# Sums of squares, transfer constants, weight layout and step sharing in a hand-scheduled attention and MoE kernel

## The chip, the cores and the metric

The kernel runs on one core of a Trainium2 chip. The metric is the device time of one execution in microseconds (us). TensorE (PE in the profile; PEld is its weight load) multiplies matrices, VectorE (DVE), ScalarE (ACT) and GpSimd (POOL) work element by element, and SyncE (SP) issues nearly all DMAs.

## The reference

For 8 batches, 8 heads, 576 positions and head size 64, q and k are mapped to 128 positive features, and linear attention is computed with them; its output goes through a feed-forward layer with an unusual gate.

```python
def phi(x):                                   # x is q or k, scaled by 64 ** -0.25
    proj = einsum('bhsd,md->bhsm', x, omega)
    sq = sum(x * x, axis=-1, keepdims=True) / 2.0
    h = proj - sq
    h = h - max(h, axis=-1, keepdims=True)
    return exp(h) / sqrt(m)
kv = einsum('bhsm,bhsd->bhmd', k_p, v);  z = sum(k_p, axis=2)
attn = einsum('bhsm,bhmd->bhsd', q_p, kv) / (einsum('bhsm,bhm->bhs', q_p, z)[..., None] + 1e-06)
h = x @ w_in                                  # x: 4608 x 512, w_in: 512 x 2048
g = h * erf(softplus(h))
out = g @ w_out                               # w_out: 2048 x 512
```

## The kernel before

The program is not written in the order in which it runs. `build` (from line 415) describes some thousands of operations: for each its name, the engines that may do it with a modelled cost and a slack for each, the tiles it reads and writes, and for some a planned time. `Plan.order` (line 161) then plays these operations through a model of the engines on the host, and the order that comes out on each engine is the order of its instructions on the chip. On the chip every engine works strictly in that order and waits where an input is not there yet, so an operation whose input is late holds everything behind it on its engine.

In the model an operation carries a due time, worked back from the planned times of the products that need it (and of the operations that need its buffers). Engines are tried in the order TensorE, ScalarE, VectorE, GpSimd, SyncE; each takes the ready operation that is due first. GpSimd takes a step that another engine may do as well only when it is due later than a slack. VectorE takes any. The names in `SHARED` (line 92) are the steps between VectorE and GpSimd: gates, splits into a high and a low part ("high", "rest"), sums of blocks and of weights, and the operands x. A DMA is modelled at lines 301 to 305: one transfer after the other at `RATE`, and landed a fixed time later. A weight fetch may be issued when it is due within `AHEAD`.

Batches follow one another. In each there are two phases (b, ph); in a phase four groups of first products (matmuls that write h, hA, hS) alternate with four of second products (o, in batches from 3 on bA and bS) of the phase before. From batch 2 on both layers use seven block products in place of eight. `starts` holds planned phase starts: 51 us for the first, then 64.5 us for each phase of batches 0 and 1, 61.3 us up to the first phase of batch 3, and 58.2 us from there on. In each phase 13.8 us are planned for attention of the next batch, spread between the products.

Attention of a batch is done for pairs of heads, two pairs (a quad) at a time. `load` (line 628) fetches u (transposed rows, for TensorE) and for each pair `un` (rows by position, 128 x 576, in one of two buffers). `un` is squared on ScalarE or GpSimd; `fold` (GpSimd, line 1200) adds halves and quarters of each row of 64 and scales, which leaves 144 numbers per partition; `sum_squares` (VectorE, line 1207) reduces these to 9 twice, once negated, into `sq`. In `project` (line 651) VectorE takes the maximum of the projection into a third place of `sq` and adds the three up (`shift`), which is the bias of the exponential on ScalarE. The first batch's pairs take another path (`load_pair`) without `fold`.

`split` (line 741) makes a batch's operands xh and xl from the attention's output, by way of differences xc; `chain` (line 873) runs softplus, erf and the gate; `operands` (line 905) makes the block operands (tiles T, gh_B, gl_B, gh_T, gl_T).

Weights are split once into high and low parts and stored in DRAM (`store`, line 458; tiles wdw, wdcSS, wdcST), then fetched into eight slots `w` of 512 KB. For the second layer a unit is stored by rows of blocks: the array is [partition, block row, block column, high or low, 256], so a row is 4 KB in one piece per partition. `column` (line 512) fetches a block column, two pieces of 2 KB (tiles wcA, wcS). `column_sums` (line 525) fetches rows (tile ct), forms sums (`make_sums`: RT, ST) and stores them again (cST to wdcST).

All instructions go through one helper, so every one has line 1064 in the profile; tiles tell them apart.

Of the kernel before, what the change touches and what calls it, by code (L numbers as in the profile page):

```python
# [11 lines left out]
F32 = mybir.dt.float32  # L12
# [6 lines left out]
ALU = mybir.AluOpType  # L19
# [4 lines left out]
P = 128  # L24
# [88 lines left out]
class Plan:  # L113
# [47 lines left out]
    def order(self, slots, caps):  # L161
# [67 lines left out]
        while True:  # L229
            progress = True  # L230
            while progress:
                progress = False
                for e in engines:
                    if not idle[e]:
                        continue
                    skipped, chosen = [], None
                    while ready[e]:
                        item = heapq.heappop(ready[e])
                        o = item[2]
                        if o.start is not None:  # L240
                            continue
                        ok = can(o)
                        if ok and e == "A":
                            if lock is not None and o.set is not None and o.macro != lock:
                                ok = False
                        if ok:
                            slack = next(s for x, _, s in o.opts if x == e)
                            if e == "S":
                                ok = o.due - now < slack
                            elif o.due - now + late < slack and slack > -1e8:  # L250
                                ok = False
                        if ok:
                            chosen = o
                            break
                        skipped.append(item)
                        if len(skipped) > 500:
                            break
                    for item in skipped:
                        heapq.heappush(ready[e], item)
                    if chosen is None:  # L260
                        continue
                    if e == "T" and half and chosen.half != half:
                        near = [x for x in ready[e] if x[2].half == half and x[2].start is None
                                and x[0] < now + NEAR and can(x[2])]
                        if near:
                            heapq.heappush(ready[e], (chosen.due, chosen.id, chosen))
                            chosen = min(near)[2]
                    o = chosen
                    progress = True
                    dur = next(c for x, c, _ in o.opts if x == e)  # L270
                    if e == "T":
                        if o.half != half:
                            dur += COST["turnout"] / 2
                        half = o.half
                        late += 0.1 * (max(0.0, now - o.due) - late)
                    if e == "V" and o.name in SHARED:

                        dur += max(0.0, until["G"] - now) % piece
                        port = now + dur
                    elif e == "G":  # L280
                        dur += max(0.0, port - now)
                        piece = dur / PIECES.get(o.name, 1) + 1e-6
                    o.eng, o.start = e, now
                    for t in o.alloc:
                        t.slot = free[t.pool].pop(0)
                        held[t.stream] += 1
                        nxt[t.stream] += 1
                    idle[e] = False
                    if e == "A":
                        if o.set is not None and o.set != table:  # L290
                            dur += COST["table"]
                            if o.set == "exp":
                                out.append("table")
                            table = o.set
                        if o.macro is not None:
                            lock = o.macro
                            if o.name.startswith("erf!"):
                                lock = None
                    out.append(o)
                    if e == "S":  # L300
                        event(now + 0.5, "idle", e)
                        begin = max(now, bw)
                        bw = begin + o.size / RATE
                        o.end = bw + 2.0
                    else:
                        o.end = until[e] = now + dur
                        event(o.end, "idle", e)
                    busy[e] += dur
                    event(o.end, "done", o)
# [43 lines left out]
        return out  # L353


RATE = 380e3
AHEAD = 40.0
AGAIN = 6
TURNS = tuple(range(0, 1000, 30))
REACH = 60.0  # L360
# [33 lines left out]
RESTS = 2.0  # L394
EARLY = (2, 0)
POW = 0
RECIP = 0.0
EARLYB = 7
PW = 1
# [15 lines left out]
def build(emit):  # L415
# [42 lines left out]
    def store(u, t):  # L458
        i = u[-1] if u[0] in "2T" else 0
        u_ = u[:-1] if u[0] in "2T" else u  # L460
        if u_ not in homes:
            homes[u_] = pl.tile("wd" + t.name, "wd" + t.name, [P, 2 if u[0] in "2T" else 1, *t.shape[1:]])
        d = homes[u_]
        stored[u] = (d, i)
        pl.op("wstore", [("S", 0.1, 1e9)], lambda e: E.fetch(d.ap[:, i], t.ap.bitcast(F32)),
              reads=[(t, (x, k)) for x in "hl" for k in range(2)], writes=[(d, i)],
              plan=clock[0] + 10.0, size=P * HW * 8)

# [30 lines left out]
    def unit(u, block=None):  # L499

        count[0] += 1
        t = pl.tile("w", "w%s_%d" % ("_".join(str(c) for c in u), count[0]),
                    [P, 2 if block is None else 1, 2, BW], F32R,
                    cap=W0 if clock[0] < starts[3] else SLOTS["w"] - CAPS["cv"] if clock[0] < starts[2 * BLOCKS2] else None)
        if u not in stored:
            make(u, t)
        else:
            d, i = stored[u]
            fetch(u, t, lambda: d.ap[:, i] if block is None else d.ap[:, i, block:block + 1])
        return t  # L510

    def column(ph, ep, wn):

        us, k = {"A11": (("2", ph, 2 * ep), 0), "A12": (("2", ph, 2 * ep), 1),
                 "A22": (("2", ph, 2 * ep + 1), 1), "S2": (("T", ph, ep, 0), 0), "S3": (("T", ph, ep, 0), 1),
                 "S1": (("T", ph, ep, 1), 0), "S4": (("T", ph, ep, 1), 1)}[wn]
        count[0] += 1
        t = pl.tile("w", f"wc{wn}{ph}{ep}_{count[0]}", [P, 2, 2, BW], F32R)
        d = homes[us]
        pl.op("wfetch", [("S", 0.1, AHEAD)], lambda e: E.fetch(t.ap.bitcast(F32), d.ap[:, :, k]),  # L520
              reads=[(d, 0), (d, 1)], writes=[(t, (x, i)) for x in "hl" for i in range(2)],
              size=P * HW * 8)
        return t

    def column_sums(ph, ep, h):
        t0, t1 = (pl.tile("w", f"ct{ph}_{ep}_{h}_{i}", [P, 2, 2, BW], F32R, "cv") for i in range(2))
        for i, t in enumerate((t0, t1)):
            d, k = stored["2", ph, 2 * ep + i, h]
            fetch(("2", ph, 2 * ep + i, h), t, lambda d=d, k=k: d.ap[:, k])
        make_sums(ph, ep, t0, t1, ("T", h))  # L530

    def make_sums(ph, fp, t0, t1, kind=("S",)):
# [95 lines left out]
    def load(m, qk):  # L628
# [6 lines left out]
        for j, x in enumerate(a["pairs"]):  # L635
# [2 lines left out]
                  writes=[(un, 0)], size=P * NC * D * 4)  # L638
            pl.op("square", [("G", 1.25, -1e9), ("A", 0.75, SQA)],
                  lambda e, un=un: E.square(e, un), reads=[(un, 0)], writes=[(un, 0)])  # L640
            pl.op("fold", [("G", 1.3, -1e9)], lambda e, un=un: E.fold(un), reads=[(un, 0)],
                  writes=[(un, 0)])
            for x_ in range(2):
                pl.op("sumsq", [("V", 0.22, -1e9)], lambda e, un=un, j=j, x_=x_: E.sum_squares(sq, un, j, x_),
                      reads=[(un, 0)], writes=[(sq, (j, x_))])
            if qk == "k":
                v = x["v"] = pl.tile("v", "v" + x["nm"], [P, (NC + 1) * D1])
                pl.op("loadv", [("S", 0.1, 1e9)], lambda e, v=v, x=x: E.v_load(v, x), writes=[(v, 0)],
# [2 lines left out]
    def project(m, qk, t0):  # L651
        a = quads[m]
        u, sq = a["u" + qk], a["sq" + qk]
        for j, x in enumerate(a["pairs"]):
            x["f" + qk] = chunked(pl.tile("f", f"f{qk}{x['nm']}", [P, NC, P]))
        mx = pl.tile("mx", f"mx{qk}{a['nm']}", [P, 2, NC])
# [390 lines left out]
def tile_attention_moe(ctx: ExitStack, tc: tile.TileContext, qT, kT, qN, kN, vP, omT, w1, w2, out):  # L1047
# [62 lines left out]
    class Emit:  # L1110
# [86 lines left out]
            else:  # L1197
                (pool if e == "G" else dve).tensor_mul(un.ap, un.ap, un.ap)

        def fold(self, un):  # L1200
            u = un.ap.rearrange("p (c d) -> p c d", d=D)
            for n in (D // 2, D // 4):
                pool.tensor_add(u[:, :, :n], u[:, :, :n], u[:, :, n:2 * n])
            u = u[:, :, :D // 4]
            pool.tensor_scalar(u, u, half_sq, 0.0, op0=ALU.mult, op1=ALU.add)

        def sum_squares(self, sq, un, j, x):
            dve.tensor_reduce(sq.ap[:, j, :, x], un.ap.rearrange("p (c d) -> p c d", d=D)[:, :, :D // 4],
                              axis=AX.X, op=ALU.add, negate=bool(x))

        def project(self, place, u, again=None):
            first = min(c for _, c in place)
# [220 lines left out]
```

## Time and profile before

| | |
|---|---|
| time, median of 3 runs | 1048.7 us (1047.02 to 1049.3) |
| time of the profiled execution | 1047.62 us |
| its span, first to last instruction | 1045.8 us |
| mean granted TensorE clock | 0.986 of 2.4 GHz |
| busy: PE, DVE, ACT, POOL | 96%, 78%, 73%, 74% |
| DMA queue q1 | 300.39 MB, 82.2% of 16 engines' span |

Busy shares are means over the whole span. TensorE's instructions overlap, so its busy share counts a matmul from its start to its modelled end; gaps shorter than one matmul are not seen in it. A bracket behind a row of a timeline is the idle time of the engine before it and what ended it.

### The profile page before, as it was taken

The page shows a single profiled execution, that of the slowest core. Times are in us where ns is not written, and L with a number is a line of the kernel's source. Part 1 is how long each engine was busy: PE and PEld are TensorE (multiplying, and loading weights), DVE is VectorE, ACT ScalarE, POOL GpSimd, SP SyncE. Part 2 cuts the span into 40 slices and gives each one's busy share as a digit, 9 for nine tenths or more (in the row PEclk, how much of TensorE's full clock was granted, in tenths as well). Part 3 has the DMA queues.
Part 4 walks back from the last instruction along what each step waited for, and adds up shares of the span by engine and source line. Part 5 has one row for each costly group of instructions (what it writes and reads, how often), then busy time and mean ns, then how long its engine had stood idle before and what let it go on. Part 6 is the DMA issues. An engine that isn't in the chain of part 4 may idle for free.

```text
span 1045.8 us, 23545 instructions
## 1 busy us (share of the span) xinstructions
PE 1001.2 (96%) x8580; PEld 961.9 (92%) x8580; DVE 815.2 (78%) x1548; ACT 759.8 (73%) x1645; POOL 770.2 (74%) x886
## 2 busy tenths in 40 slices
PE   7899999999999999999899999999999999999998
PEld 6798889989999999999899999999998999989997
DVE  4778898897867688775887979779796869776855
ACT  6879888877787577875687868677687767665542
POOL 6849698889777575763787969599785858685745
PEclk9899899999999999999999999999999999999999
DMA  9476677889779898888798899878988768889996
GB/s 253 151 263 239 232 243 275 311 298 332 259 258 315 311 368 307 327 302 264 264 349 304 290 325 338 294 252 307 360 287 322 241 216 316 283 322 310 341 323 212
DMA packets 114114, 302.41 MB, mean 289 GB/s; under 512 B 10768, under 2 KB 16336, under 8 KB 114000
## 3 DMA queue, kind: packets, MB, share of 16 engines
q1 hardware_dynamic: 113680, 300.39, 82.2%
q8 instruction: 68, 1.11, 0.4%
q10 hardware_dynamic: 320, 0.52, 0.2%
q14 instruction: 46, 0.38, 0.1%
HBM read 257.88 MB, written 42.99 MB: 288 GB/s over the span
## 4 chain that ended last, share of the span: by engine, by line
PE 61%; DMA 16%; POOL 9%; DVE 7%; ACT 3%; issue 2%; SPq 1%; POOLq 0%; ACTq 0%; DVEq 0%
PE hA L1064 13%; PE o L1064 9%; PE h L1064 8%; PE bA L1064 8%; PE bS L1064 6%; PE hS L1064 5%; PE nd L1064 4%; DMA unq<-qN 3%; PE ppk L1064 3%; POOL xl L1064 3%; PE kvp L1064 2%; PE pt L1064 2%; DMA w<-wdw 2%; DMA wdcST<-cST 2%; POOL hq L1064 2%
## 5 line engine op out<-in xcount | busy, mean ns | idle before, releaser
L1064 POOL TENSOR_TENSOR hq<-gs,hq 128x288 f32<-128x288 f32 x162 | 155.7, 988 | 70.2 <-ACT gs L1064 69.9
L1064 PE MATMUL o<-gh,w 128*128 128x288 f32 x768 | 172.0, 303 | 4.9 <-DVE os L1064 3.3
L1064 PE MATMUL hA<-xh,w 128*128 128x288 f32 x576 | 148.8, 301 | 3.9 <-DMA w<-wdw 2.2
L1064 PEld LDWEIGHTS o<-gh,w 128*128 128x128 f32 x768 | 129.4, 191 | 8.8 <-DVE os L1064 3.8
L1064 PE MATMUL h<-xh,w 128*128 128x288 f32 x512 | 121.0, 312 | 4.8 <-DVE w L1064 3.7
L1064 ACT ACT_TABLE_LOAD x92 | 118.0, 1283 | 2.9 <-PEq L1424 1.3
L1064 PE MATMUL o<-gl,w 128*128 128x288 f32 x384 | 114.2, 297 | 0.0
L1064 ACT ACTIVATE fk<-ppk,mxk 128x128 f32<-128x128 f32 x288 | 78.3, 407 | 44.6 <-DVE mxk L1064 44.6
L1064 PE MATMUL hS<-xh,wS 128*128 128x288 f32 x384 | 107.2, 299 | 2.9 <-ACT hq L1064 1.3
L1064 PEld LDWEIGHTS hA<-xh,w 128*128 128x128 f32 x576 | 103.3, 189 | 6.3 <-DMA w<-wdw 1.8
L1064 POOL TENSOR_TENSOR unq<-unq 128x288 f32<-128x288 f32 (+2 forms) x63 | 51.7, 822 | 73.4 <-ACT unq L1064 58.0
L1064 PE MATMUL hA<-xh,wS 128*128 128x288 f32 x384 | 103.0, 302 | 2.6 <-DVE hq L1064 1.3
L1064 PEld LDWEIGHTS h<-xh,w 128*128 128x128 f32 x512 | 87.7, 193 | 8.0 <-issue 2.9
L1064 ACT ACTIVATE hq<-hA 128x288 f32<-128x288 f32 x95 | 39.6, 417 | 67.2 <-PE hA L1064 67.0
L1064 PE MATMUL hA<-xl,w 128*128 128x288 f32 x288 | 85.1, 296 | 0.0
L1064 POOL TENSOR_SCALAR wt<-st 128x512 f16<-128x512 f32 (+2 forms) x74 | 61.4, 846 | 25.3 <-DMA st<-w 21.6
L1064 ACT ACTIVATE fq<-ppq,mxq 128x128 f32<-128x128 f32 x288 | 77.8, 412 | 2.6 <-DVE mxq L1064 2.3
L1064 ACT ACTIVATE gs<-hq 128x576 f32<-128x576 f32 x128 | 78.8, 675 | 0.4
L1064 PE MATMUL bA<-gh_B,wcA 128*128 128x288 f32 x320 | 78.3, 299 | 0.5 <-DMA wcA<-wdw 0.5
L1064 ACT ACTIVATE gs<-gs 128x576 f32<-128x576 f32 x128 | 78.2, 674 | 0.4
L1064 PE MATMUL h<-xl,w 128*128 128x288 f32 x256 | 76.8, 300 | 0.5 <-DVE xl L1064 0.5
L1064 PE MATMUL bS<-gh_T,wcS 128*128 128x288 f32 x320 | 75.5, 299 | 1.3 <-DMA wcS<-wdcST 1.3
(175 smaller groups left out, 3438.3 us busy)
## 6 DMA issues: line engine op xcount, KB each, us to landing
w<-wdw SPq DMA_DIRECT2D x96, 512.0 KB, 6.4
wS<-wdcSS SPq DMA_DIRECT2D x96, 512.0 KB, 6.6
wcS<-wdcST SPq DMA_DIRECT2D x80, 512.0 KB, 6.4
wcA<-wdw SPq DMA_DIRECT2D x60, 512.0 KB, 5.4
st<-w SPq DMA_DIRECT2D x32, 512.0 KB, 5.0
wdw<-w SPq DMA_DIRECT2D x32, 512.0 KB, 3.5
w<-wdw SPq DMA_DIRECT2D x48, 256.0 KB, 5.1
v<-vP SPq DMA_DIRECT2D x32, 325.0 KB, 5.6
```

The source lines that it names most:

```text
L1064: return tc.keep_in_program_order(method(*args, **kwargs))
```

## The change

- The fold on GpSimd goes. VectorE sums all 64 squares of a row in one reduction of 128x576 per `un` tile, in place of two of 128x144. A new GpSimd step `signs`, once per quad and per q or k, writes the scaled and negated sums (two operations on 128x18 numbers).
- `RATE` goes from 380e3 to 350e3 bytes per us, the fixed time after a transfer from 2.0 to 3.4 us (`DLAT`), `AHEAD` from 40 to 60 us.
- The second layer's weights are stored with the block column outside, so a column is one piece of 4 KB per partition and a row two of 2 KB.
- In the model VectorE no longer takes a step in `SHARED` that another engine may do too, while it is due more than `VNEAR` = 25 us ahead.

```diff
--- before.py
+++ after.py
@@ -249,6 +249,8 @@
                                 ok = o.due - now < slack
                             elif o.due - now + late < slack and slack > -1e8:
                                 ok = False
+                            elif e == "V" and o.name in SHARED and len(o.opts) > 1 and o.due - now > VNEAR:
+                                ok = False
                         if ok:
                             chosen = o
                             break
@@ -301,7 +303,7 @@
                         event(now + 0.5, "idle", e)
                         begin = max(now, bw)
                         bw = begin + o.size / RATE
-                        o.end = bw + 2.0
+                        o.end = bw + DLAT
                     else:
                         o.end = until[e] = now + dur
                         event(o.end, "idle", e)
@@ -353,8 +355,9 @@
         return out
 
 
-RATE = 380e3
-AHEAD = 40.0
+RATE = 350e3
+DLAT = 3.4
+AHEAD = 60.0
 AGAIN = 6
 TURNS = tuple(range(0, 1000, 30))
 REACH = 60.0
@@ -394,6 +397,7 @@
 RESTS = 2.0
 EARLY = (2, 0)
 POW = 0
+VNEAR = 25.0
 RECIP = 0.0
 EARLYB = 7
 PW = 1
@@ -459,10 +463,10 @@
         i = u[-1] if u[0] in "2T" else 0
         u_ = u[:-1] if u[0] in "2T" else u
         if u_ not in homes:
-            homes[u_] = pl.tile("wd" + t.name, "wd" + t.name, [P, 2 if u[0] in "2T" else 1, *t.shape[1:]])
+            homes[u_] = pl.tile("wd" + t.name, "wd" + t.name, [P, 2, 2, 2, BW] if u[0] in "2T" else t.shape)
         d = homes[u_]
         stored[u] = (d, i)
-        pl.op("wstore", [("S", 0.1, 1e9)], lambda e: E.fetch(d.ap[:, i], t.ap.bitcast(F32)),
+        pl.op("wstore", [("S", 0.1, 1e9)], lambda e: E.fetch(d.ap[:, :, i] if u[0] in "2T" else d.ap, t.ap.bitcast(F32)),
               reads=[(t, (x, k)) for x in "hl" for k in range(2)], writes=[(d, i)],
               plan=clock[0] + 10.0, size=P * HW * 8)
 
@@ -506,7 +510,7 @@
             make(u, t)
         else:
             d, i = stored[u]
-            fetch(u, t, lambda: d.ap[:, i] if block is None else d.ap[:, i, block:block + 1])
+            fetch(u, t, lambda: d.ap[:, :, i] if u[0] == "2" else d.ap if block is None else d.ap[:, block:block + 1])
         return t
 
     def column(ph, ep, wn):
@@ -517,7 +521,7 @@
         count[0] += 1
         t = pl.tile("w", f"wc{wn}{ph}{ep}_{count[0]}", [P, 2, 2, BW], F32R)
         d = homes[us]
-        pl.op("wfetch", [("S", 0.1, AHEAD)], lambda e: E.fetch(t.ap.bitcast(F32), d.ap[:, :, k]),
+        pl.op("wfetch", [("S", 0.1, AHEAD)], lambda e: E.fetch(t.ap.bitcast(F32), d.ap[:, k]),
               reads=[(d, 0), (d, 1)], writes=[(t, (x, i)) for x in "hl" for i in range(2)],
               size=P * HW * 8)
         return t
@@ -526,7 +530,7 @@
         t0, t1 = (pl.tile("w", f"ct{ph}_{ep}_{h}_{i}", [P, 2, 2, BW], F32R, "cv") for i in range(2))
         for i, t in enumerate((t0, t1)):
             d, k = stored["2", ph, 2 * ep + i, h]
-            fetch(("2", ph, 2 * ep + i, h), t, lambda d=d, k=k: d.ap[:, k])
+            fetch(("2", ph, 2 * ep + i, h), t, lambda d=d, k=k: d.ap[:, :, k])
         make_sums(ph, ep, t0, t1, ("T", h))
 
     def make_sums(ph, fp, t0, t1, kind=("S",)):
@@ -638,11 +642,8 @@
                   writes=[(un, 0)], size=P * NC * D * 4)
             pl.op("square", [("G", 1.25, -1e9), ("A", 0.75, SQA)],
                   lambda e, un=un: E.square(e, un), reads=[(un, 0)], writes=[(un, 0)])
-            pl.op("fold", [("G", 1.3, -1e9)], lambda e, un=un: E.fold(un), reads=[(un, 0)],
-                  writes=[(un, 0)])
-            for x_ in range(2):
-                pl.op("sumsq", [("V", 0.22, -1e9)], lambda e, un=un, j=j, x_=x_: E.sum_squares(sq, un, j, x_),
-                      reads=[(un, 0)], writes=[(sq, (j, x_))])
+            pl.op("sumsq", [("V", 0.68, -1e9)], lambda e, un=un, j=j: E.sum_squares(sq, un, j),
+                  reads=[(un, 0)], writes=[(sq, (j, 0))])
             if qk == "k":
                 v = x["v"] = pl.tile("v", "v" + x["nm"], [P, (NC + 1) * D1])
                 pl.op("loadv", [("S", 0.1, 1e9)], lambda e, v=v, x=x: E.v_load(v, x), writes=[(v, 0)],
@@ -651,6 +652,8 @@
     def project(m, qk, t0):
         a = quads[m]
         u, sq = a["u" + qk], a["sq" + qk]
+        pl.op("signs", [("G", 0.4, -1e9)], lambda e: E.signs(sq), reads=[(sq, (j, 0)) for j in range(2)],
+              writes=[(sq, (j, x)) for j in range(2) for x in range(2)])
         for j, x in enumerate(a["pairs"]):
             x["f" + qk] = chunked(pl.tile("f", f"f{qk}{x['nm']}", [P, NC, P]))
         mx = pl.tile("mx", f"mx{qk}{a['nm']}", [P, 2, NC])
@@ -1197,16 +1200,12 @@
             else:
                 (pool if e == "G" else dve).tensor_mul(un.ap, un.ap, un.ap)
 
-        def fold(self, un):
-            u = un.ap.rearrange("p (c d) -> p c d", d=D)
-            for n in (D // 2, D // 4):
-                pool.tensor_add(u[:, :, :n], u[:, :, :n], u[:, :, n:2 * n])
-            u = u[:, :, :D // 4]
-            pool.tensor_scalar(u, u, half_sq, 0.0, op0=ALU.mult, op1=ALU.add)
-
-        def sum_squares(self, sq, un, j, x):
-            dve.tensor_reduce(sq.ap[:, j, :, x], un.ap.rearrange("p (c d) -> p c d", d=D)[:, :, :D // 4],
-                              axis=AX.X, op=ALU.add, negate=bool(x))
+        def sum_squares(self, sq, un, j):
+            dve.tensor_reduce(sq.ap[:, j, :, 0], un.ap.rearrange("p (c d) -> p c d", d=D), axis=AX.X, op=ALU.add)
+
+        def signs(self, sq):
+            for x, sign in ((1, -half_sq), (0, half_sq)):
+                pool.tensor_scalar(sq.ap[:, :, :, x], sq.ap[:, :, :, 0], sign, 0.0, op0=ALU.mult, op1=ALU.add)
 
         def project(self, place, u, again=None):
             first = min(c for _, c in place)
```

## Rows read from the trace of the kernel before

**Rows 1.** Page, part 1: busy time, share of the span, instructions.
```profile
PE 1001.2 (96%) x8580; PEld 961.9 (92%) x8580; DVE 815.2 (78%) x1548; ACT 759.8 (73%) x1645; POOL 770.2 (74%) x886
```

**Rows 2.** Stretches of PE: from:to, length, busy (matmuls), granted clock, DMA share, GB/s.
```profile
24.00:35.00 11.00, 6.69 (x29) 0.69 0.59 190
...
100.00:113.00 13.00, 9.25 (x47) 0.74 0.70 235
...
463.00:472.00 9.00, 7.17 (x39) 0.81 1.00 388
...
497.00:506.00 9.00, 6.36 (x37) 0.81 0.90 357
...
564.00:568.00 4.00, 2.52 (x19) 1.00 0.95 358
...
683.00:690.00 7.00, 4.75 (x25) 0.76 0.73 279
...
805.00:813.00 8.00, 5.85 (x34) 0.79 0.60 221
```

**Rows 3.** Chain that ended last, 660 to 695: start, length, what.
```profile
666.45 6.93 DMA unq<-qN
...
677.21 5.11 POOL xl L1064 x6
682.33 1.53 POOL xc L1064 x2
```

**Rows 4.** Timeline of POOL, 655 to 690: start, length, operation, idle before.
```profile
674.17 1.80 POOL L1064 TENSOR_TENSOR unq<-unq 128x288 f32<-128x288 f32 x2 [12.53 <-ACT unq L1064]
...
676.45 0.76 POOL L1064 TENSOR_SCALAR xh<-xc 128x576 fp32r<-128x576 f32 x1
```

**Rows 5.** Waits: who waited for whom, us in total, times, longest.
```profile
POOL unq L1064 <- ACT unq L1064: 58.0, 8, 12.8
...
ACT unq L1064 <- DMA unq<-qN: 26.8, 12, 3.3
```

**Rows 6.** Chain that ended last, 440 to 505.
```profile
459.07 6.40 DMA ct<-wdw
...
489.96 7.36 DMA ct<-wdw
```

**Rows 7.** Groups by form: engine, operation, tiles, shapes, count, busy, mean ns, idle before.
```profile
L1064 POOL TENSOR_TENSOR unq<-unq 128x288 f32<-128x288 f32 x28 | 26.0, 929 | 58.9 <-ACT unq L1064 58.0
...
L1064 POOL TENSOR_TENSOR unq<-unq 128x144 f32<-128x144 f32 x28 | 17.3, 618 | 2.2
...
L1064 DVE TENSOR_REDUCE sqq<-unq 128x9 f32<-128x144 f32 x56 | 14.0, 294 | 3.6 <-POOL unq L1064 3.5
...
L1064 POOL TENSOR_SCALAR unq<-unq 128x144 f32<-128x144 f32 x28 | 11.5, 412 | 2.5
```

**Rows 8.** Instructions on tile sqq: count, ns min/median/max, first and last start.
```profile
L1064 DVE TENSOR_REDUCE sqq<-ppq x84: 540/548/560, 66.3 to 864.6; 128x3 f32<-128x384 f32 x84
```

**Rows 9.** DMA issues: tiles, queue, count, KB each, median us to landing.
```profile
w<-wdw SPq DMA_DIRECT2D x96, 512.0 KB, 6.4
...
wcA<-wdw SPq DMA_DIRECT2D x60, 512.0 KB, 5.4
```

**Rows 10.** Timeline of DVE, 92 to 115.
```profile
103.94 1.34 DVE L1064 TENSOR_TENSOR gl<-hq,gh 128x576 fp32r<-128x576 f32 x1
```

**Rows 11.** Timeline of PE, 100 to 108.
```profile
106.75 0.58 PE L1064 MATMUL h<-xh,w 128*128 128x288 f32 x1 [2.67 <-DVE w L1064]
```

**Rows 12.** Instructions on tile gs: count, ns min/median/max, first and last start.
```profile
L1064 POOL TENSOR_TENSOR hq<-gs,hq x162: 784/815/1347, 86.3 to 1012.7; 128x288 f32<-128x288 f32 x162
...
L1064 DVE TENSOR_TENSOR hq<-gs,hq x47: 745/1062/1409, 84.7 to 1014.6; 128x576 f32<-128x576 f32 x47
```

**Rows 13.** Instructions on tiles o and bA: count, ns min/median/max, first and last start.
```profile
L1064 PE MATMUL o<-gh,w x768: 288/295/513, 122.0 to 509.8; 128*128 128x288 f32 x192
...
L1064 PE MATMUL bA<-gh_B,wcA x320: 288/295/401, 521.7 to 1037.5; 128*128 128x288 f32 x160
```

## The prediction

> **What bounds the kernel now.** I read the page's busy times first. TensorE is busy 1001.2 of 1045.8 us; the other three have a fifth to a quarter of the span free [rows 1]. So the most that any new order can bring is what TensorE loses: 44.6 us without a matmul, and the time at the lower clock. No engine's total matters by itself; only a step that comes too late for TensorE does.
>
> The second view is TensorE's stretches around its longest stops [rows 2]. In each row, length less busy time is idle, and length times (1 - granted clock) is what the lower level, 1.2 in place of 2.4 GHz, took on top. That gives four places:
> - 564 to 568, 683 to 690, 805 to 813: idle 1.48 + 2.25 + 2.15 = 5.9, clock 0 + 1.7 + 1.7 = 3.4; together 9.3 us. Batches 4, 5 and 6 lose them at the same point of the batch.
> - 463 to 472 and 497 to 506: idle 1.83 + 2.64 = 4.5, clock 1.7 + 1.7; together 7.9 us.
> - 100 to 113: idle 3.75, clock 3.4; together 7.1 us.
> - 24 to 35: idle 4.31, clock 3.4; together 7.7 us, in the first batch's pairs.
>
> The third view is the chain of waits at each place. Before 686 us it runs over a load of unq (6.93 us), its square on ScalarE, its fold on GpSimd, then 5.11 us of xl and 1.53 us of xc on GpSimd [rows 3]. GpSimd's own timeline shows it idle for 12.53 us before that fold: it stands in its queue for data that are late, with the operands of the next batch behind it, and it is 2.28 us from the fold's start (674.17) to the first of these (676.45) [rows 4]. Over the run GpSimd waits 58.0 us in 8 such places for ScalarE's square, which itself waits 26.8 us for the load [rows 5]. At 463 and 497 us the chain ends in a fetch of ct, 6.40 and 7.36 us, with VectorE's sums (and the evacuations that TensorE needs) queued behind it [rows 6]. At 106.75 us TensorE has waited 2.67 us for VectorE to write a weight tile [rows 11], while VectorE did a gl of 1.34 us that a much later product needs [rows 10].
>
> **The fold.** It takes from GpSimd, for q, 26.0 + 17.3 + 11.5 = 54.8 us in 28 tiles; k has as many tiles of the same shapes, so an estimate for both is 110 us. VectorE loses 112 reductions of 128x144 at 0.294 us, 32.9 us [rows 7]. It gains 56 of 128x576, a size that the trace doesn't have. From 144 numbers (0.294) to 384 (0.548 [rows 8]) is 1.06 ns a number; 192 more give 0.75 us. The input of the larger row is in PSUM, of the smaller in SBUF, so I bound it by 0.65 and 0.85. 56 x 0.75 = 42.0, which is 9 us more on VectorE (3.5 to 15), beside 230 us in which it is free. The signs add 56 operations on 128x18 numbers to GpSimd. The nearest row is 0.412 us for 128x144, mostly for 8 times the numbers; I take 0.25, at least 0.1: 14 us (6 to 23). GpSimd so gets back some 95 us, 12% of its work.
>
> What of this lies on the path: at the three places of batches 4 to 6, the 2.28 us of fold between the late square and the operands. That is about the idle time of each of them (1.48, 2.25, 2.15), and with the idle the fall of the clock goes. Against it stands the signs' own wait: if signs come in the fold's place in GpSimd's queue, GpSimd still stands there until VectorE has summed the late tile, 0.75 us in place of 2.28. Also `un` is free again for the next load some 2 us earlier. I take 7.5 of the 9.3 us; bounds 0 and 9.3.
>
> [...]
>
> **The transfer constants.** A 512 KB fetch was modelled to land 0.5 MB / 380e3 + 2.0 = 3.4 us after an undisturbed issue; it is now 4.9 us. Measured is 6.4 in the median, queueing included [rows 9]. So the order is made for arrivals that are 1.5 us nearer to the truth, and steps that wait for a load are put later in the queues of ScalarE, VectorE and GpSimd, with other work ahead of them. Nothing moves faster by it: what lands at 465.5 lands there still. At the two ct places the fetch took 3.0 and 4.0 us more than was modelled; 1.5 of it is now foreseen. I take half of the 7.9 us, 4; bounds -4 (a new order puts another queue's head there) and 7.9. At 24 to 35 no `fold` and no weight sum runs; I take 0, from -3 to 7.7. `AHEAD` changes little where the eight slots w set when a fetch can start, as they do once TensorE eats a slot in 12 matmuls: 0.
>
> **The weight layout.** 140 column fetches lose their second piece (140 x 128 = 17920 fewer packets); 32 row fetches, 16 ct, 16 stores of rows and 16 of wdcST gain one (10240 more). Bytes don't change. Columns in two pieces land in 5.4 us, rows in one in 6.4 [rows 9]: a second piece is not seen in the landing. I take 0; bounds -1 and 2 us, since in the last 100 us a slot's wait for its fetch does reach TensorE.
>
> **Late shared steps.** They free VectorE for what is urgent. The gl at 103.94 belongs to a product that the plan has at 51 + 64.5 + 64.5/4 = 131.6 us. It was due some 27 us later, so VectorE would leave it. 1.34 of the 2.67 us of TensorE's wait go [rows 10, 11]; with a part of the clock I take 2 of 7.1 (bounds 0 and 7.1). The cost: a gate on GpSimd is two pieces of 815 ns, 1.63 us, against 1.06 on VectorE [rows 12]. The room for it is the fold's 95 us. What VectorE left comes back to it within 25 us of its due time, in bunches. How near that is to the real need depends on where TensorE stands: its first o is at 122.0, against the plan's 131.6, 10 us early; its first bA at 521.7 against 492.9 + 14.5 = 507.4, 14 us late [rows 13]. So the margin is 15 us in the first phases and 39 later. I charge 3 us for new stops; bounds 0 and 20. The signs' hop between VectorE's sum and `shift`, 28 times, is mostly under attention's slack: 1 us, bounds 0 and 4.
>
> **The sum** against the profiled execution: 1047.6 - 7.5 - 4 - 2 + 3 + 1 = 1038.1 us. The median of the runs is 1.1 above that execution: 1039.2, rounded to 1039.
>
> **The rivals.**
> - Stops move, nothing is won. Signs inherit the wait of 12.5 us [rows 4], GpSimd's room fills with shared steps, and x waits as before. For it: a new order of thousands of steps makes new stops as easily as it removes old ones. The 13.5 us gained are spent on three new stops of 4.4 us (2.64 idle and 1.7 clock, as at 497 [rows 2]): 1048.
> - Slower: VectorE's waiting for 25 us makes gates and low parts late in batches 0 to 2, where TensorE runs ahead of the plan and GpSimd also makes weight tiles. The price of one such stop is 4.4 to 7.1 us [rows 2]. It decides from the third stop on; five at 4.4 give 1047.6 - 13.5 + 22 + 1.1 = 1057. Against it: [rows 13] leave 15 us even there.
> - All four places go: 9.3 + 7.9 + 7.1 + 7.7 = 32 us, 1048.7 - 32 = 1017.
> - The change doesn't do what it says: the reduction takes 0.85 or more and GpSimd's signs 0.4. That costs engines which aren't the bound, and stays within the forecast.
>
> **Chances.** Forecast (1024 to 1046) 0.55, no change (1046.6 to 1050.8) 0.15, slower 0.25, all places 0.05. 0.2%, about 2 us, is what a measurement of this kernel can tell. Faster 0.60, same 0.15, slower 0.25. The parts' bounds reach from 1049 - 32 to 1049 + 20; for 8 in 10 I cut at 1022 below and go to the slower rival's 1057 above.
>
> **What would show it.** No unq group on GpSimd but the squares; VectorE reductions of 128x576 near 0.75 us; GpSimd's wait for ScalarE's unq gone from the waits, and none as large on VectorE's sums; no stop of TensorE after xl and xc in batches 4 to 6; the granted clock above 0.986; ct fetches no longer ahead of VectorE's evacuations; more gates on GpSimd than 162 halves. Wrong it would be if GpSimd waits for sums as long as it did for squares, or if TensorE waits for gates, gh or gl before 320 us.

## The result and the profile after

The changed kernel takes 1020.6 us in the median (1019.43 to 1022.14), the kernel before 1047.9 beside it: ratio 0.9741, interval 0.9719 to 0.9763. The prediction was 1039, from 1022 to 1057: the direction was right, the gain of 27 us nearly three times the forecast, and the time lies below the range. The profiled execution of the changed kernel took 1019.43 us, its span is 1017.6.

The busy times, which answer to [rows 1]:

```profile
PE 985.3 (97%) x8580; PEld 952.5 (94%) x8580; DVE 744.3 (73%) x1399; ACT 761.0 (75%) x1634; POOL 813.2 (80%) x982
```

The span is 28.2 us shorter. TensorE's time outside its matmuls fell from 44.6 to 1017.6 - 985.3 = 32.3 us, 12.3 less. The mean granted clock rose from 0.986 to 0.996, which is 1045.8 x 0.014 - 1017.6 x 0.004 = 10.6 us. What the lower level is in the trace: from 687 to 689 us of the kernel before the granted clock is 0.50 and matmuls of 288 columns start 0.24 us apart, 1.2 columns a ns; from 640 to 642 us it is 1.00 and they start 0.13 us apart. The other 5.3 us were not located; gaps shorter than a matmul, which its busy time hides, would fit, but no row shows them. GpSimd is busier than before by 43 us, though the fold is gone: it took over the shared steps that VectorE left. VectorE is less busy by 71.

Stretches of TensorE in the changed kernel (from:to, length, busy, granted clock, DMA share, GB/s), beside [rows 2]. The first is the first batch's pairs; the next three hold its longest new stops:

```profile
24.00:35.00 11.00, 7.07 (x74) 1.00 0.79 257
140.00:150.00 10.00, 8.05 (x50) 0.83 0.81 281
165.00:176.00 11.00, 7.94 (x51) 0.84 0.84 258
345.00:350.00 5.00, 2.99 (x22) 1.00 0.81 252
```

And two wider stretches, batch 3 with its fetches of ct and batches 4 to 6 with the making of x; first before, then after:

```profile
430.00:510.00 80.00, 75.53 (x647) 0.96 0.82 288
...
570.00:690.00 120.00, 117.62 (x1039) 0.99 0.89 306
690.00:810.00 120.00, 117.02 (x1042) 1.00 0.87 306
```

```profile
430.00:510.00 80.00, 79.92 (x694) 1.00 0.92 331
...
570.00:690.00 120.00, 119.60 (x1078) 1.00 0.90 318
690.00:810.00 120.00, 119.53 (x1070) 1.00 0.89 313
```

Length less busy time gives the idle time. That of batch 3's stretch fell from 4.47 to 0.08 us, of batches 4 to 6 from 2.38 + 2.98 to 0.40 + 0.47, and the granted clock after is 1.00 in all three. Around 145 and 170 us TensorE still stops for a weight tile of VectorE, as it did in [rows 11]; the timeline of the changed kernel shows it:

```profile
145.95 0.40 PE L1067 MATMUL h<-xh,w 128*128 128x288 f32 x1 [1.80 <-DVE w L1067]
```

```profile
170.75 0.61 PE L1067 MATMUL o<-gh,w 128*128 128x288 f32 x1 [3.02 <-DVE w L1067]
```

How GpSimd now meets the operands x in batch 5, to be held against [rows 4] (start, length, operation, idle before):

```profile
651.96 0.52 POOL L1067 TENSOR_SCALAR sqk<-sqk 128x18 f32<-128x18 f32 x2
...
656.26 0.94 POOL L1067 TENSOR_SCALAR xh<-xc 128x576 fp32r<-128x576 f32 x1 [2.15 <-PE hA L1067]
```

It waits 2.15 us there for a buffer, in place of 12.53 for a late square. What the engines wait for, to [rows 5]:

```profile
POOL unq L1067 <- DMA unq<-qN: 23.3, 5, 8.4
...
POOL sqk L1067 <- DVE sqk L1067: 14.0, 6, 4.7
...
ACT unq L1067 <- DMA unq<-qN: 8.4, 7, 2.8
...
DVE RT L1067 <- DMA ct<-wdw: 6.0, 3, 4.4
```

The 58.0 us for ScalarE's squares are gone, and ScalarE's own wait for the load fell from 26.8 to 8.4. The new operations (count, ns min/median/max, first and last start):

```profile
L1067 DVE TENSOR_REDUCE sqq<-unq x28: 734/742/755, 28.3 to 797.1; 128x9 f32<-128x576 f32 x28
L1067 POOL TENSOR_SCALAR sqq<-sqq x28: 220/223/765, 32.8 to 798.3; 128x18 f32<-128x18 f32 x28
```

And the gates, to [rows 12]:

```profile
L1067 POOL TENSOR_TENSOR hq<-gs,hq x238: 786/812/1346, 79.9 to 986.4; 128x288 f32<-128x288 f32 x119
...
L1067 DVE TENSOR_TENSOR hq<-gs,hq x9: 747/860/1368, 309.3 to 990.1; 128x576 f32<-128x576 f32 x9
```

119 of 128 gates run on GpSimd, where it was 81.

### The profile page after: what moved, and what is told of

Same layout as the page of the kernel before. It is cut to its first block, busy times and chain, and to the rows that moved or that the text cites. A ratio compares the mean times of both kernels' runs of the same rounds, so it can differ in the third digit from the quotient of the medians.

```text
span 1017.6 us, 23486 instructions
## 1 busy us (share of the span) xinstructions
PE 985.3 (97%) x8580; PEld 952.5 (94%) x8580; DVE 744.3 (73%) x1399; ACT 761.0 (75%) x1634; POOL 813.2 (80%) x982
## 4 chain that ended last, share of the span: by engine, by line
PE 75%; POOL 8%; DVE 5%; DMA 5%; ACT 4%; issue 2%; SPq 1%; DVEq 0%; ACTq 0%; POOLq 0%
PE hA L1067 17%; PE o L1067 11%; PE bA L1067 10%; PE bS L1067 8%; PE h L1067 7%; PE hS L1067 7%; PE nd L1067 4%; PE ppk L1067 3%; PE kvp L1067 3%; POOL hq L1067 3%; PE pt L1067 3%; PE ppq L1067 2%; POOL wt L1067 2%; DMA w<-wdw 1%; DMA uk<-kT 1%
## 5 line engine op out<-in xcount | busy, mean ns | idle before, releaser
L1067 POOL TENSOR_TENSOR hq<-gs,hq 128x288 f32<-128x288 f32 x238 | 208.6, 904 | 43.4 <-ACT gs L1067 43.4
L1067 PE MATMUL h<-xh,w 128*128 128x288 f32 x512 | 118.4, 309 | 3.0 <-DVE w L1067 2.2
L1067 PE MATMUL hS<-xh,wS 128*128 128x288 f32 x384 | 105.1, 298 | 1.3 <-ACT hq L1067 0.9
L1067 PE MATMUL hA<-xh,wS 128*128 128x288 f32 x384 | 100.7, 298 | 1.2 <-DVE hq L1067 1.2
L1067 ACT ACTIVATE hq<-hA 128x288 f32<-128x288 f32 x84 | 34.3, 410 | 66.0 <-PE hA L1067 65.6
L1067 POOL TENSOR_TENSOR gl_B<-hq,gh_B 128x288 fp32r<-128x288 f32 x90 | 77.8, 890 | 1.2 <-PE hA L1067 0.5
L1067 POOL TENSOR_TENSOR gl<-hq,gh 128x288 fp32r<-128x288 f32 x82 | 72.8, 916 | 5.4 <-ACT gh L1067 4.2
L1067 DVE TENSOR_TENSOR hq<-hA,hq 128x288 f32<-128x288 f32 x96 | 43.5, 454 | 45.7 <-PE hA L1067 37.6
```

Of the source, the lines that this page charges most:

```text
L1067: return tc.keep_in_program_order(method(*args, **kwargs))
```

## The experiments

### Theories and all results

Theory A: the fold, in GpSimd's queue ahead of the next batch's operands. Theory B: the model's arrivals of transfers. Theory C: luck, any new order being faster or slower by chance. Theory D: late shared steps keep VectorE free. Each part was taken from the changed kernel alone ("u_") and put into the kernel before alone ("o_"). Ratios are to the kernel before, run beside each; us are the ratio's difference from 1 on 1048 us. The kernels with u_, a_ and best_ have the new weight layout, except u_layout; those with o_ and b_ the old.

| kernel | sums | constants | late steps | ratio (95%) | us |
|---|---|---|---|---|---|
| after | new | new | yes | 0.9741 (0.9719 to 0.9763) | -27 |
| u_sums | old | new | yes | 0.9811 (0.9787 to 0.9835) | -20 |
| u_const | new | old | yes | 1.0029 (0.9992 to 1.0065) | +3 |
| u_layout (old layout) | new | new | yes | 0.9758 (0.9728 to 0.9788) | -25 |
| u_late | new | new | no | 0.9696 (0.9673 to 0.9719) | -32 |
| o_sums | new | old | no | 0.9821 (0.9777 to 0.9864) | -19 |
| o_const | old | new | no | 0.9902 (0.9865 to 0.9940) | -10 |
| o_late | old | old | yes | 1.0101 (1.0060 to 1.0142) | +11 |
| b_nofold | fold left out | old | no | 0.9866 (0.9818 to 0.9915) | -14 |
| a_jit1 | new | new | yes | 0.9664 (0.9594 to 0.9735) | -35 |
| a_jit2 | new | new | yes | 0.9731 (0.9672 to 0.9791) | -28 |
| b_jit1 | old | old | no | 1.0035 (0.9992 to 1.0077) | +4 |
| b_jit2 | old | old | no | 1.0191 (1.0123 to 1.0258) | +20 |
| best_jit1 | new | new | no | 0.9753 (0.9734 to 0.9771) | -26 |
| best_jit2 | new | new | no | 0.9780 (0.9763 to 0.9796) | -23 |
| best_ahead40 | new | new, look-ahead 40 | no | 0.9679 (0.9663 to 0.9695) | -34 |
| best_dlat2 | new | old, look-ahead 60 | no | 0.9843 (0.9809 to 0.9877) | -16 |
| best_dlat5 | new | fixed time 5.4 | no | 1.0142 (1.0050 to 1.0233) | +15 |
| o_const_jit1 | old | new | no | 0.9920 (0.9877 to 0.9963) | -8 |

### One part taken away

u_sums: the fold and the two small reductions as before. u_const:

```diff
-                        o.end = bw + DLAT
+                        o.end = bw + 2.0
...
-RATE = 350e3
-DLAT = 3.4
-AHEAD = 60.0
+RATE = 380e3
+AHEAD = 40.0
```

u_layout: the second layer's weights stored by rows again, and u_late:

```diff
-                            elif e == "V" and o.name in SHARED and len(o.opts) > 1 and o.due - now > VNEAR:
-                                ok = False
```

> The changed kernel with the fold on GpSimd and the two small reductions put back; constants, layout and late shared steps stay. Theory A (the fold on the way from a late load to the next batch's operands costs what the stops of batches 4 to 6 cost): 9 to 12 us of the 27 us come back, about 1031 us, and TensorE stops again after xl and xc. Theory B (the model's later arrivals are what removed those stops): 2 us or less come back, 1020 to 1023. Theory C (any new order gives a time somewhere between 1015 and 1050, whatever the edit): nothing can be said beforehand.

> The changed kernel with the old transfer rate, the old fixed time and the old look-ahead; sums, layout and late shared steps stay. Theory A: the fetches of ct hold VectorE again and some 8 to 10 us come back, about 1030 us. Theory B: 15 us or more come back, 1036 us or more. Theory C: anything from 1015 to 1050.

> The changed kernel with the second layer's weights stored by rows again, in the same order of instructions on every engine. By the prediction a second piece of a fetch costs nothing that reaches TensorE: 1019 to 1022 us. If the layout brought part of the 17 us that were not forecast, column fetches land later than 5.8 and 5.3 us and the time is over 1024.

> The changed kernel in which VectorE takes any shared step at once, as before; sums, constants and layout stay. Theory A (late steps are worth 2 us less 3 for new stops): within 3 us of the changed kernel. Rival D (late steps keep VectorE free for evacuations everywhere, and that is the part that was not forecast): 8 us or more come back, 1028 or more, with VectorE's busy time up by some 70 us.

Taking the constants away loses the whole gain and more (30 us), as theory B expected. Taking the fold's removal away loses 7, less than theory A's 9 to 12 and more than B's 2. The layout is worth nothing that can be told. Without late steps the kernel is 5 us faster, which neither A (within 3 us) nor D (slower) expected. The layout is seen only in SyncE's time to issue a transfer. Here is a column fetch with the old layout (u_layout), then with the new one (after):

```profile
L1067 SPq DMA_DIRECT2D wcA<-wdw x60: 517/524/650, 496.6 to 993.1; - x60
```

```profile
L1067 SPq DMA_DIRECT2D wcA<-wdw x60: 319/320/910, 499.2 to 993.5; - x60
```

### One part alone, and the fold left out in place

The first three put one part of the change into the kernel before. b_nofold keeps every engine's order and leaves the fold's operations out:

```diff
 def fold(self, un):
     u = un.ap.rearrange("p (c d) -> p c d", d=D)
-    for n in (D // 2, D // 4):
-        pool.tensor_add(u[:, :, :n], u[:, :, :n], u[:, :, n:2 * n])
-    u = u[:, :, :D // 4]
-    pool.tensor_scalar(u, u, half_sq, 0.0, op0=ALU.mult, op1=ALU.add)
```

> The kernel before with the new sums alone. Theory A (fold on the way of the operands): 8 to 12 us less than before, about 1037 us, TensorE's stops in batches 4 to 6 gone. Theory B (the constants carry the gain, and the sums are worth 7 us only where arrivals are foreseen): within 4 us of before.

> The kernel before with the new transfer constants alone; fold, layout and sharing as before. Theory B: 15 to 25 us less than before, 1022 to 1032 us, with GpSimd's wait of 58 us for ScalarE's squares cut to under 30. Theory A: about 8 us less, 1040 us. Theory E (constants and late shared steps must come together): within 3 us of before.

> The kernel before with late shared steps alone. After the run in which taking them away from the changed kernel gained 6 us: slower than before by 3 to 10 us, 1050 to 1057, since GpSimd then has the fold and the shared steps too. The prediction's account (2 us gained, 3 lost): within 3 us of before.

> The kernel before, in its own order on every engine, in which the fold's three operations are left out and the two small reductions sum a quarter of the squares (that part of the sum is left out). It tells what GpSimd's time in the fold costs when nothing else moves. Theory A: the 2.28 us ahead of the operands go in batches 4 to 6, and GpSimd doesn't stand for the late square at all, so the three stops go: 9 us less than before, 1038 us. Rival: the operands wait for something else right behind it, 0 to 3 us less.

b_nofold is the clean one, since every engine keeps its order: 14 us less (9 to 19). GpSimd's timeline in it, at the place of [rows 4]:

```profile
663.05 0.93 POOL L1064 TENSOR_SCALAR xh<-xc 128x576 fp32r<-128x576 f32 x1 [11.02 <-PE hA L1064]
```

GpSimd stands there for 11 us again, but now because it is ahead of its time and TensorE has yet to give a buffer free. The operands x start at 663.05 in place of 676.45 us. Of these 13.4 us, 9.0 had been gained earlier, as the first bA shows beside [rows 13] (512.7 against 521.7):

```profile
L1064 PE MATMUL bA<-gh_B,wcA x320: 288/295/401, 512.7 to 1019.4; 128*128 128x288 f32 x160
```

So leaving the fold out brought x 4.4 us forward at this place, and half of the 18.1 us by which this execution leads at the last bA (1019.4 against 1037.5) was won ahead of batches 4 to 6. The profiled execution, of 1029.5 us, is 7 us faster than the kernel's median. TensorE idles half as long in batches 4 to 6, as the table below shows.

The sums alone gain 19 us and the constants alone 10, less than the 15 to 25 that theory B expected. The idle time of TensorE, length less busy in the same two stretches as above (each row is one profiled execution; that of u_const was 9 us faster than its median, that of a_jit1 9 us slower):

| kernel | fold | constants | 430 to 510 | 570 to 810 |
|---|---|---|---|---|
| before | yes | old | 4.5 | 5.4 |
| b_jit1 | yes | old | 2.7 | 11.0 |
| b_jit2 | yes | old | 3.4 | 11.7 |
| o_late | yes | old | 7.7 | 9.7 |
| o_const | yes | new | 2.3 | 5.4 |
| o_const_jit1 | yes | new | 1.7 | 1.2 |
| u_sums | yes | new | 0.2 | 5.7 |
| o_sums | no | old | 4.1 | 2.2 |
| b_nofold | no | old | 3.2 | 2.8 |
| u_const | no | old | 5.9 | 3.2 |
| best_dlat2 | no | old | 2.4 | 3.2 |
| after | no | new | 0.1 | 0.9 |
| a_jit1 | no | new | 0.4 | 0.7 |
| a_jit2 | no | new | 0.7 | 2.3 |
| u_late | no | new | 1.3 | 1.2 |
| best_jit1 | no | new | 1.8 | 1.1 |
| best_jit2 | no | new | 1.3 | 1.9 |

(The kernels called jit and best are explained below; best_dlat5, made for transfers 2 us slower, is apart.) The left column is 2.4 or more with the old constants and 2.3 or less with the new ones. The right column is 3.2 or less without the fold and 5.4 or more with it, with one exception: o_const_jit1 has the fold and idles 1.2 us, in an order that differs from o_const's only by small random moves. So taking the fold out is not the only way to clear these batches. The rows of two that have one part each, o_const first, then o_sums, and the two later stretches of o_const_jit1:

```profile
430.00:510.00 80.00, 77.72 (x689) 1.00 0.85 307
570.00:690.00 120.00, 118.70 (x1054) 1.00 0.87 308
690.00:810.00 120.00, 115.93 (x1031) 1.00 0.89 305
```

```profile
430.00:510.00 80.00, 75.86 (x655) 0.97 0.84 286
570.00:690.00 120.00, 119.05 (x1065) 1.00 0.87 311
690.00:810.00 120.00, 118.72 (x1056) 1.00 0.87 308
```

```profile
570.00:690.00 120.00, 119.61 (x1067) 1.00 0.89 312
690.00:810.00 120.00, 119.18 (x1067) 1.00 0.88 310
```

Nor are o_const's 5.4 us the stops of the kernel before. TensorE no longer stops for x at 686 and 808; its longest stops in these batches are at 756 and 778 us, the first of them behind two folds, for which VectorE's sums waited:

```profile
756.31 0.40 PE L1065 MATMUL hA<-xh,w 128*128 128x288 f32 x1 [1.92 <-DVE hq L1065]
```

What the constants act by is read from who waits for loads. In o_const, and below it in o_sums:

```profile
ACT unq L1065 <- DMA unq<-qN: 4.7, 2, 2.9
...
DVE RT L1065 <- DMA ct<-wdw: 0.4, 1, 0.4
```

```profile
POOL sqk L1063 <- DVE sqk L1063: 45.0, 12, 8.4
...
ACT unq L1063 <- DMA unq<-qN: 25.4, 13, 4.3
...
DVE RT L1063 <- DMA ct<-wdw: 12.9, 6, 4.3
```

With the old constants ScalarE's wait for unq is 12.2 to 27.3 us and VectorE's for ct 10.3 to 24.4, over the eight kernels that have them. Over the eleven kernels with the new 3.4 us they are 3.6 to 13.7 and 0.4 to 14.9. The ranges overlap at their ends (12.2 in b_jit2 against 13.7 in a_jit2, and the 14.9 for ct in best_jit1). The signs' wait, a rival of the prediction, is there as well: 45.0 us in o_sums, and 53.2 in u_late, one of the fastest kernels here:

```profile
POOL sqk L1064 <- DVE sqk L1064: 53.2, 12, 9.8
```

So a wait of that size can cost little; what stands behind it in each place was not traced.

o_late is slower by 11 us, where 3 to 10 were expected. GpSimd then has the fold and most shared steps:

```profile
PE 997.1 (94%) x8580; PEld 962.2 (91%) x8580; DVE 716.8 (68%) x1440; ACT 757.3 (72%) x1611; POOL 922.3 (87%) x1165
```

### How far an order's luck goes

The same contents, with the due times shaken:

```diff
-NUDGES = {
-}
+NUDGES = {i: (1000 + i, 0.5) for i in range(34)}
```

(second seed: 2000.)

> The changed kernel, with every due time moved by up to 0.5 us at random every 30 us of the model (first seed): the same contents, another order. If an order's luck is small, within 3 us of 1020. If it is large (theory C), off by 5 us or more, and differences of that size between the other runs say nothing of their edit.

> As the run before, second seed: within 3 us of 1020 if luck is small, 5 us or more off it if luck is large.

> The kernel before, moved in the same way, first seed. Small luck: within 3 us of 1048. Large luck: off by 5 us or more; if it falls below 1042, a part of the 27 us was that the order before was a poor draw.

> As the run before, second seed: within 3 us of 1048, or 5 us or more off it.

Three orders of the changed contents give 0.9664, 0.9731 and 0.9741, three of the contents before 1, 1.0035 and 1.0191. So luck is up to 8 us in the one and 20 us in the other, as far as three orders show it, and theory C holds for differences of that size between single orders: the 7 us of u_sums and the 10 us of o_const are of that size. The 27 us stand above it, for the two groups don't touch. The kernel before is the fastest of its three orders and the changed kernel the slowest of its three, so luck did not make the gain.

### Late steps, the look-ahead and the modelled time

All four start from u_late. best_jit1 and best_jit2 shake it as above; the other two change a constant each:

```diff
-AHEAD = 60.0
+AHEAD = 40.0
```

```diff
-RATE = 350e3
-DLAT = 3.4
+RATE = 380e3
+DLAT = 2.0
```

> Sums, constants and layout without late steps (1014 us), every due time moved by up to 0.5 us at random, first seed. If late steps cost 6 us beyond luck, it is again 4 us or more below the changed kernel moved by the same seed (1012.7), so 1009 or less. If it was luck: anywhere from 1012 to 1022.

> The same with the second seed. Late steps cost beyond luck: 1015 or less (changed kernel, same seed: 1019.2). Luck: anywhere from 1012 to 1022.

> Sums, constants and layout without late steps, with the look-ahead back at 40 us. The prediction says the look-ahead does nothing where slots set a fetch's start: 1011 to 1018 us. If the look-ahead carries the constants' gain: 1024 or more.

> Sums and layout without late steps, with the look-ahead at 60 us and the old rate and fixed time, so that the model has arrivals early again. If foreseen arrivals carry the constants' gain: 1025 to 1035 us (the sums alone gave 1030). If the look-ahead carries it: 1011 to 1018.

Without late steps the three orders give 0.9696, 0.9753 and 0.9780, with them 0.9664, 0.9731 and 0.9741. The 5 us by which u_late was faster are no more than an order's luck; whether late steps help by 3 us or not at all can't be told from these. The look-ahead does nothing (0.9679 against 0.9696). The modelled time does it: with the old one the gain falls by half against u_late (15 us), by 7 against the slowest order with the new one, and the waits are back. That is one order, so the size is open by luck:

```profile
ACT unq L1064 <- DMA unq<-qN: 27.3, 12, 4.3
DVE RT L1064 <- DMA ct<-wdw: 24.4, 12, 4.6
```

### The modelled time moved on, and the constants alone once more

```diff
-DLAT = 3.4
+DLAT = 5.4
```

(in u_late; o_const_jit1 is o_const shaken by the first seed.)

> Sums, constants and layout without late steps, with the fixed time after a transfer at 5.4 us in place of 3.4. If a margin helps as such: 1010 us or less. If what helps is that the model has it right: 1014 to 1025, since slots are then modelled as taken for too long.

> The kernel before with the new constants alone, due times moved at random by the first seed. If the constants' 10 us stand above luck: 1042 or less, against 1048.6 for the kernel before with the same move. If not: 1042 to 1060.

A fixed time of 5.4 us costs 47 us against 3.4, more than any luck seen here, so it is no margin that helps. Neither expectation named so slow a kernel. ScalarE's waits for loads are nearly gone (last row), but others are large:

```profile
POOL sqk L1064 <- DVE sqk L1064: 63.0, 13, 8.5
...
POOL sqq L1064 <- DVE sqq L1064: 25.3, 8, 6.9
...
ACT unq L1064 <- DMA unq<-qN: 1.2, 1, 1.2
```

TensorE loses most of it in two stretches, before 310 us and from 510 to 690 (6.8 and 6.7 us idle from 510 to 570 and from 570 to 690):

```profile
510.00:570.00 60.00, 53.19 (x452) 0.94 0.77 277
570.00:690.00 120.00, 113.35 (x992) 1.00 0.88 313
```

Why the order that is made for such arrivals is so much worse wasn't settled: the rows show where, not why. The constants alone, shaken, are at 0.9920 against 1.0035 for the kernel before with the same move, 12 us, like the 10 us unshaken. Both orders with the new constants are faster than all three with the old.

## Why the prediction was wrong

**Its causes held in the main.** Taking the fold out in place and correcting the arrivals each gained time, and each goes with less idle time in the stretch for which the prediction had named it, with the exception of o_const_jit1. That the two make up the whole gain isn't shown: the parts alone give 19 + 10 - 11 = 18 of 27 us.

**The step that failed is what of each cause lies on TensorE's path: too few places were counted.**

**The fold's term was too small.** 7.5 us were taken, bounded by 9.3, from three stops of batches 4 to 6. Measured are 14 us (9 to 19) in place and 19 as the first part; the 7 as the last part are of the size of an order's luck. Two things were wrong. At the place of [rows 4] the term took 2.28 us of fold; without it x came 4.4 us earlier, since GpSimd no longer stood for the late square. And it looked at batches 4 to 6 alone, while b_nofold had won 9.0 of its 18.1 us before them. Of the 58.0 us of waiting for squares [rows 5], 25.8 lie before these three places, between 67 and 486 us. Which of the early waits held TensorE wasn't traced.

The reduction's price was right: 742 ns for 750 forecast. The signs took 223 ns in the median for 250, within their bounds. That no wait as large would stand on VectorE's sums held in the changed kernel (14.0 us), but as a sign it told little: u_late has 53.2 and is faster.

**The constants' term was the one most mis-sized.** It was 4 us of 7.9, half of the two ct stops; measured are 10 alone, 12 alone with both kernels shaken, 15 with the sums (7 to 17 against the four orders with the new time), 30 with late steps as well. Each of these is open by an order's luck, but all lie above 4. The half itself was near what the ct stops gave: in o_const the idle time of their stretch fell from 4.47 to 2.28 us and the granted clock rose from 0.96 to 1.00. What failed is that the term looked at ct alone, though ScalarE's 26.8 us of waiting for unq stood among the rows, and fell to 4.7. In o_const TensorE's idle time fell elsewhere too, from 2.3 to 0.4 us between 510 and 570, where the first of the fold's stops had been, and from 5.2 to 3.4 between 810 and 1000.

The look-ahead and the layout were rightly put at nothing. A fetch of ct, a row in two pieces now, lands later, 7.9 us against 6.0 in the median, but it takes 7.4 in u_layout, with one piece and the same order, so most of that is the order's.

**The late steps' terms, -2 and +3, were about right.** Three orders with and three without can't be told apart. The expected gain at the weight tiles didn't come: stops for VectorE's w remain at 145 and 170 us, 1.80 + 3.02 us and 1.7 + 1.8 of clock, 8.3 in place of the 7.1 before. New stops like that at 348 us (2.0) are there as charged. Late steps alone were 11 us slower (o_late), and 22 beside the sums (o_sums to u_const), about as much as luck in the old contents; with the new arrivals they cost nothing that can be told. The slower rival's place, the early batches, was not where o_late lost: it idles 7.7 us between 430 and 510. In the changed contents it is hinted at: between 100 and 200 us TensorE idles 8.2, 6.8 and 5.5 us in the three orders with late steps, 2.3, 3.7 and 5.2 in the three without.

**The range.** All four places together were given 1017 and a chance of 0.05, as if four independent strokes of luck were needed. One new order, made with better arrivals and less work on GpSimd, removed two of them whole. The third, 24 to 35, had its clock lifted (granted 1.00, idle 3.9), but u_layout, in the same order, was granted 0.84 there, and the mean granted clock of the changed kernel's own four runs goes from 0.990 to 0.996, so the order alone doesn't settle it. The prediction's reason for 0 at that place, that no fold runs there, was not exact: one of unq runs from 33.8 us, after both of TensorE's stops. The cut at 1022, inside the parts' own bounds of 32 us down, left the time outside. On the other side, an order's luck of 8 to 20 us would have asked for a range of that width by itself.

What stays open: how much of the interplay of late steps with the constants (11 and 22 us lost without them, 10 gained in u_sums against o_const, 3 at most in the changed kernel) is more than luck. The fastest contents seen, 0.9664 to 0.9696 (a_jit1, best_ahead40, u_late), differ from the changed kernel by no more than an order's luck.

## What to carry to other kernels

Where engines run a fixed order, an operation that waits for a late transfer holds what stands behind it in its queue (here the operands x behind 12.53 us of waiting on GpSimd [rows 4]); find it as a long idle time ahead of a cheap step, and either move that step to a queue with nothing urgent behind it or correct the arrival that the order was made for. Correct it to what the trace shows; here 2 us more cost 47. Before reading a few microseconds into one edit of such a schedule, shake the order without changing its contents and see how far the time moves by itself.

## What the hardware showed beside that

SyncE took 524 ns to issue a fetch of wcA, 512 KB, in two pieces per partition (u_layout) and 320 ns in one piece (the changed kernel), in the median of 60 of each; ct, which went the other way, took 564 ns in two pieces (the changed kernel) and 380 in one (u_layout), in the median of 16 of each, in the same order. None of it can be told in the kernel's time (ratio 0.9758 in u_layout, 0.9741 in the changed kernel, with overlapping intervals).
